# Residual add in the last two batches: token rows by 32x32 turns and DRAM in place of TensorE

## Chip, cores and metric

The kernel runs on one core of a Trainium2 chip. The metric is the device time of one execution in microseconds, the median of the runs shown. All inputs and outputs lie in the chip's DRAM at the start and the end.

## What is computed

For x of shape (8, 3136, 256), a filter in the frequency domain is applied along the sequence, and a low-rank mixer and a two-layer channel network with a residual follow:

```
X = rfft(x, axis=1);  y = irfft(X * (filt_r + i*filt_i), n=3136, axis=1)
yt = y.transpose(0, 2, 1)                      # (8, 256, 3136)
u  = y + (yt @ U @ V).transpose(0, 2, 1)       # U: 3136x32, V: 32x3136
out = u + relu(u @ w_ch1) @ w_ch2              # 256 -> 1024 -> 256, fp32 out
```

The change concerns the first `u +` of the last line.

## The kernel before, in words

**Layout of u.** Stage `s4` leaves u of a batch in the tile `ut[b]`, 128 partitions x (2 halves of the model dimension) x 3136 tokens, in fp16: the model dimension lies on the partitions. The first layer wants it so. The output, and so the residual, wants tokens on the partitions.

**Channel network.** The 8 x 3136 tokens are cut into 49 groups of 512 (`Group`, number n from 0 to 48); a group may straddle two batches (its `seg` list). `mm1(gr, t)` (L487) makes hidden tile t of 8: two matmuls of 512 columns into a PSUM bank of tag "m", and ScalarE applies the relu (L490). `mm2(gr, t)` (L510) does four matmuls of 256 columns into `gr.pc`, a bank of tag "o" (there are two of them). Two values of t finish one block of 128 tokens; on the second, `residual` (L502) adds u to the same PSUM block with two matmuls of 128 columns that take a piece of `ut` as the weights and the identity as the moving operand: this turns u and adds it at once. After two blocks (t = 3 and t = 7) VectorE (DVE) copies the bank into `och` (L517); after t = 7 GpSimd's queue (POOL) stores 512 KB to the output (L522), and in the last group the SP queue stores each half (L519).

**Order of work.** The program order is written out by hand. The main loop makes 392 steps, step 8n+t being `mm1(groups[n], t)`, then `mm2(groups[n-1], t)`, then whatever generators `plan[8n+t]` lists. The residual and the copy of group n thus come in the steps of group n+1. After the loop there are eight more `mm2` for group 48, without `mm1`. `plan` holds the preparation of batch b, spread over the steps in which batch b-1 is in the channel network:

- `f1s`: the first transform; in the steps before group 37 for the last batch.
- `mids`: 13 items, each one a matmul `pz` (L383, L385) into a bank of tag "z" (four of them), a DVE multiply with the filter into `uv` (L391), after every second item a DVE subtract and add (L395, L396), and, three items later, a matmul `pe` on `uv` (L344, function `s3`), a ScalarE cast into `e` (L354) and, for every second pair, a store to DRAM (`ct<-e`, L363, SP queue). For batch 7 items 7 to 12 have their `pz` in steps 297, 299, 301, 303, 305 and 307; the `pe` of items 7 to 9 come in steps 303, 305 and 307, those of items 10 to 12 in steps 310, 311 and 312.
- `loads`: the three parts of `ct` come back as `eb` (L415, SP queue), for batch 7 in steps 309, 310 and 315.
- `ranks`: a chain of small matmuls and four DVE copies (L437), steps 314 to 319.
- `s4s`: matmuls `pu` (L455) on `eb`, cast into `ut` by DVE (L462) and ScalarE (L460), steps 322 to 334 for batch 7.

Each engine's queue and the SP queue run in program order, and semaphores release them. Group 37 starts at step 296; batch 6 starts inside group 36, batch 7 inside group 42 (448 tokens of batch 6, 64 of batch 7). So in groups 37 to 41 the preparation of batch 7 runs beside the network, and in groups 42 to 48 nothing does.

Of the kernel before, what the change touches and what calls it, by code (L numbers as in the profile page):

```python
# [10 lines left out]
F16 = mybir.dt.float16  # L11
# [7 lines left out]
DM = 256  # L19
RANK = 32  # L20
NH = 1024
GT = 512
NG = NB * SEQ // GT

# [53 lines left out]
def kernel(  # L80
# [11 lines left out]
    nc = tc.nc  # L92
# [15 lines left out]
    sb = ctx.enter_context(tc.tile_pool(name="sb", bufs=1))  # L108
    ps = ctx.enter_context(tc.tile_pool(name="ps", bufs=2, space=bass.MemoryType.PSUM))

    def bank(tag, name, dtype=F32):

        return ps.tile([128, 512 if dtype == F32 else 1024], dtype, tag=tag, bufs=4 if tag == "z" else 2, name=name)

    def dram(t, off, dims):
        return bass.AP(tensor=t, offset=off, ap=[list(d) for d in dims])
# [88 lines left out]
    tu = eb[0:RANK, 0:12, :].rearrange("p r d -> p (r d)")  # L205
    tu0 = cst.tile([RANK, NR], F16)

    def u_hat():
        for n in range(8):
            pu = bank("zmzo"[n % 4], "puh")  # L210
            for i in range(4):
                j = 4 * n + i
                nc.tensor.matmul(pu[0:RANK, 98 * i:98 * i + 98], usb[:, j, :], ws[:, j * 98:j * 98 + 98],
                                 start=(i == 0), stop=True, skip_group_check=True)
            copy = nc.vector.tensor_copy if n % 2 else nc.scalar.copy
            copy(tu.rearrange("p (k c j) -> p k c j", c=4, j=32)[:, :, :, 4 * n:4 * n + 4],
                 view(pu[0:RANK], 0, [[1, 24], [24, 4], [98, 4]]))
            copy(view(tu0, 32 * (n // 2 % 2) + 8 * (n // 4) + 4 * (n % 2), [[1, 4], [16, 2]]), view(pu[0:RANK], 96, [[98, 4], [1, 2]]))
# [42 lines left out]
    def unread(p, n, size=512):  # L261
        for _ in range(n):
            nc.tensor.matmul(p[:, 512 - size:512], m64[:, 0:128], m64[:, 0:size], start=True, stop=True, skip_group_check=True)
# [154 lines left out]
    def rank(b):  # L418
        ph = bank("z", "ph")
        for i in range(24):  # L420
            c = i % 4
            nc.tensor.matmul(ph[32 * c:32 * c + 32, 0:DM], uh[:, i + (3 if b == 0 and i > 21 else 1), :], e3[b, i // 4][:, i % 4, :],  # L422
                             start=(i < 4), stop=(i >= 20 and c != 0))
            if b == 0 and i == 19:
                yield
        nc.tensor.matmul(ph[0:32, 0:DM], uh[:, 0, :], e3[b, 6], start=False, stop=True)
        hp = sb.tile([128, DM], F16, tag="hp", bufs=1, name="hp")
        nc.scalar.copy(hp, ph[:, 0:DM])
        if b:
            yield  # L430
        pk = bank("z", "pk")
        nc.tensor.matmul(pk[:, 0:DM], kr, hp, start=True, stop=True)
        h1 = sb.tile([RANK, DM], F16, tag="h1", bufs=2, name="h1")
        nc.scalar.mul(h1, pk[0:32, 0:DM], 2 / 49)  # L434
        yield
        for g in range(4):
            nc.vector.tensor_copy(eb[0:32, 16 * g:16 * g + 16, :],  # L437
                                  bass.AP(tensor=h1.tensor, offset=h1.offset, ap=[[h1.ap[0][0], 32], [0, 16], [1, DM]]))
            yield
# [4 lines left out]
    def s4(b):  # L444
        ut[b] = sb.tile([128, 2, NQ, NR], F16, tag="ut", bufs=2, name="ut")
        for n in range(8):
            g = 2 * (n % 4) + n // 4
            for dh in range(2):
                tag = (("m", "o"), ("z", "z"))[n % 2][dh] if b == 0 else "z"
                pu = bank(tag, "pu")  # L450
                if b == 0:
                    unread(pu, 1, 120)
                d = slice(128 * dh, 128 * dh + 128)
                for i in range(8):
                    nc.tensor.matmul(pu[:, NQ * i:NQ * i + NQ], eb[:, 8 * n + i, d], sv[:, 8 * g + i, :],  # L455
                                            start=(i == 0), stop=True, skip_group_check=True)
                dst = ut[b][:, dh, :, 8 * g:8 * g + 8]
                src = pu[:, 0:8 * NQ].rearrange("p (r q) -> p q r", q=NQ)
                if dh and (b == 0 or n % 2):
                    nc.scalar.copy(dst, src)  # L460
                else:
                    nc.vector.tensor_copy(dst, src)  # L462
                yield
# [13 lines left out]

    groups = [Group(n) for n in range(NG)]

    def utv(b):  # L480
        return ut[b].rearrange("p h q r -> p h (q r)")

    def mm1(gr, t):
        ph = bank("m", "phh")
        for b, t0, o, n in gr.seg:
            for dh in range(2):
                nc.tensor.matmul(ph[:, o:o + n], w1sb[:, dh, 128 * t:128 * t + 128], utv(b)[:, dh, t0:t0 + n],  # L487
                                 start=(dh == 0), stop=(dh == 1), skip_group_check=True)
        h = sb.tile([128, 512], F16, tag="h16", bufs=17, name="h16")
        nc.scalar.activation(h, ph, RELU)  # L490
        gr.h.append(h)

    def residual(gr, o, i):
        last = []
        for b, t0, so, n in gr.seg:
            a, z = max(so, 128 * i), min(so + n, 128 * i + 128)
            for dh in range(2):
                if a < z:
                    p = a - 128 * i
                    last.append((o[p:p + z - a, 128 * dh:128 * dh + 128], utv(b)[:, dh, t0 + a - so:t0 + z - so], dh))  # L500
        for d, w, dh in last:
            nc.tensor.matmul(d, w, idn, start=False, stop=(dh == 1), skip_group_check=True)  # L502

    def mm2(gr, t):
        i, half = t // 2, t % 2
        if t % 4 == 0:
            gr.pc = bank("o", "pc")
        o = gr.pc[:, 256 * (i % 2):256 * (i % 2) + 256]
        for tt in range(4 * half, 4 * half + 4):
            nc.tensor.matmul(o, gr.h[tt][:, 128 * i:128 * i + 128], w2sb[:, tt, :],  # L510
                             start=(tt == 0), stop=False, skip_group_check=True)
        if half:
            residual(gr, o, i)
        if t % 4 == 3:
            if t == 3:
                gr.och = sb.tile([128, 4, DM], F32, tag="och", bufs=2, name="och")
            nc.vector.tensor_copy(gr.och[:, i - 1:i + 1, :], gr.pc.rearrange("p (j d) -> p j d", d=DM))  # L517
            if gr.n == NG - 1:
                nc.sync.dma_start(dram(out.tensor, (gr.n * GT + 128 * (i - 1)) * DM, [[DM, 128], [128 * DM, 2], [1, DM]]),  # L519
                                  gr.och[:, i - 1:i + 1, :])  # L520
            elif t == 7:
                nc.gpsimd.dma_start(dram(out.tensor, gr.n * GT * DM, [[DM, 128], [128 * DM, 4], [1, DM]]), gr.och)  # L522


    S = [8 * (b * SEQ // GT) for b in range(NB)] + [8 * NG]
    plan = [[] for _ in range(8 * NG)]

    def deal(gen, count, a, z):
        for i in range(count):
            plan[max(0, int(a + i * (z - a) / count))].append(gen)  # L530
# [6 lines left out]
    mids = [mid(0, "o")] + [mid(b) for b in range(1, NB)]  # L537
    ranks = [rank(b) for b in range(NB)]
    s4s = [s4(b) for b in range(NB)]

    u_hat()
    u_ordered()
# [48 lines left out]
    for b in range(1, NB):  # L591
        a, z = S[b - 1], S[b]
        e = z - (17 if b == 1 else 20 if b < 6 else 22)
# [8 lines left out]
        if b + 1 < NB:  # L602
            for c in range(4):
                plan[a + (9 + 2 * c if b == 1 else 1 + 4 * c)].append(later_x(b + 1, c))
            deal(f1s[b + 1], 16, a + (21 if b == 1 else 10), z - (13 if b == 1 else 20))

    for n, gr in enumerate(groups):
        for t in range(8):
            mm1(gr, t)
            if n:  # L610
                mm2(groups[n - 1], t)
            for gen in plan[8 * n + t]:
                next(gen, None)
    for t in range(8):
        mm2(groups[-1], t)
# [30 lines left out]
```

## Time and profile before

| what | value |
|---|---|
| median of 3 runs | 520.44 us (519.37 to 521.15) |
| the profiled execution | 522.24 us, of which span 520.5 us |
| TensorE clock granted (mean) | 0.993 of full speed |
| TensorE matmuls (PE) busy | 497.2 us, 96% of the span |
| TensorE weight loads (PEld) busy | 355.4 us, 68% |
| VectorE (DVE) busy | 352.3 us, 68% |
| ScalarE (ACT) busy | 377.1 us, 72% |
| GpSimd (POOL) busy | 80.7 us, 15% |
| DMA moved | 88.22 MB, mean 170 GB/s |

Busy time is the union of an engine's instructions over the span of one profiled execution. Matmuls are pipelined: the duration shown for one is longer than the time after which the next can start, so the distance between starts is the better measure of what a matmul takes. Weight loads (PEld) overlap matmuls. In answers of the trace the first number of a line is the start in us from the beginning of the span, the second the length; brackets give the idle time before it and what ended it. The group numbers and steps above are matched to times by the shapes of the matmuls (group 42's `mm1` is cut into 448 and 64 columns).

### The profile page before, as it was taken

To read this page: it belongs to the slowest core of one execution; us is meant where nothing else is said; L and a number is where in the kernel's file an instruction comes from. 1 tells how busy PE (TensorE), PEld (TensorE's weight loads), DVE (VectorE), ACT (ScalarE), POOL (GpSimd) and SP (SyncE) were. 2 spreads that over 40 slices of the span, in tenths; PEclk is the share of its full clock that TensorE was granted. 3 is DMA by queue.
4 is the path that set the end of the run, shared out by engine and by line. 5 is a ranking of instruction groups with operands and counts; after the bars stand their busy time and mean duration, and the time that the engine had idled before them with its cause. 6 is when DMAs were issued, how large, how long until landed. Compare 5 with 4: busy or idle time off the path is not lost.

```text
span 520.5 us, 11966 instructions
## 1 busy us (share of the span) xinstructions
PE 497.2 (96%) x4852; PEld 355.4 (68%) x4852; DVE 352.3 (68%) x469; ACT 377.1 (72%) x704; POOL 80.7 (15%) x122
## 2 busy tenths in 40 slices
PE   4887899999999999999999999899999999999997
PEld 4545556776767776777767777577667766776665
DVE  5886698588847974788747974689745995621112
ACT  6875779767985789668976799467985677666662
POOL 6662010111010120111010110012010010101110
PEclk9998999999999999999999999899999999999999
DMA  8997846758685586828684597618875136212113
GB/s 194 179 216 175 151 110 188 234 198 171 181 265 206 117 222 207 273 87 185 180 275 180 130 236 218 239 42 196 235 232 199 62 134 189 107 42 83 81 42 122
DMA packets 67375, 88.22 MB, mean 170 GB/s; under 512 B 4835, under 2 KB 51875, under 8 KB 67320
## 3 DMA queue, kind: packets, MB, share of 16 engines
q0 software_dynamic: 14704, 41.58, 30.8%
q1 hardware_dynamic: 52616, 45.88, 28.8%
q8 instruction: 38, 0.62, 0.5%
q14 instruction: 17, 0.14, 0.1%
HBM read 55.20 MB, written 47.78 MB: 198 GB/s over the span
## 4 chain that ended last, share of the span: by engine, by line
PE 82%; DMA 8%; DVE 4%; ACT 2%; issue 1%; POOL 1%; SPq 0%; POOLq 0%; DVEq 0%; ACTq 0%
PE pc L510 31%; PE phh L487 30%; PE pu L455 5%; PE pc L502 4%; PE pf L249 4%; PE pe L344 4%; PE pz L383 3%; DVE uv L391 2%; DMA ct<-e 2%; DMA w2sb<-in_moe_w_ch_dram 2%; DMA x<-in_x_dram 2%; DMA eb<-ct 2%; PE ph L422 1%; DMA fab<-in_filt_i_dram 1%; POOL x L127 1%
## 5 line engine op out<-in xcount | busy, mean ns | idle before, releaser
L490 ACT ACTIVATE h<-phh 128x512 f16<-128x512 f32 x392 | 235.9, 603 | 90.3 <-PE phh L487 88.8
L510 PE MATMUL pc<-w2sb,h 128*128 128x256 f16 x1568 | 234.9, 273 | 0.4 <-DMA w2sb<-in_moe_w_ch_dram 0.4
L487 PE MATMUL phh<-ut,w1sb 128*128 128x512 f16 (+7 forms) x896 | 233.9, 353 | 0.4 <-DVE ut L462 0.4
L510 PEld LDWEIGHTS <-h 128*128 128x128 f16 x1568 | 151.7, 97 | 91.8 <-issue 1.5
L517 DVE COPY och<-pc 128x512 f32<-128x512 f32 x98 | 67.6, 690 | 99.5 <-PE pc L502 98.2
L391 DVE TENSOR_TENSOR uv<-pz,fab 128x1024 f16<-128x1024 f32 (+1 forms) x104 | 120.8, 1179 | 12.6 <-PE pz L383 10.4
L522 POOL DMA_DIRECT2D out_dram<-och x48 | 39.0, 813 | 408.2 <-DVE och L517 392.5
L487 PEld LDWEIGHTS <-w1sb 128*128 128x128 f16 x896 | 77.5, 97 | 19.2 <-issue 1.5
L354 ACT CAST e<-pe 128x512 f16<-128x512 f32 x96 | 56.5, 591 | 19.4 <-PE pe L344 18.8
L462 DVE CAST ut<-pu 128x392 f16<-128x392 f32 x92 | 48.8, 560 | 23.8 <-PE pu L455 22.2
L254 ACT CAST asb<-pf 98x512 f16<-98x512 f32 x96 | 57.2, 598 | 0.2
L502 PE MATMUL pc<-idn,ut 128*128 128x128 f16 (+1 forms) x400 | 54.2, 220 | 0.0
L437 DVE COPY eb<-h 32x4096 f16<-32x4096 f16 x32 | 38.2, 1232 | 14.2 <-ACT h L434 14.1
L455 PE MATMUL pu<-sv,eb 97*128 97x49 f16 x1024 | 40.8, 188 | 4.8 <-DMA eb<-ct 4.8
L344 PE MATMUL pe<-uv,m 128*128 128x512 f16 (+1 forms) x117 | 41.3, 371 | 2.4 <-DVE uv L391 1.3
L455 PEld LDWEIGHTS <-eb 97*128 97x128 f16 x1024 | 37.8, 98 | 6.2 <-DVE eb L437 3.1
L502 PEld LDWEIGHTS <-ut 128*128 128x128 f16 (+1 forms) x400 | 38.2, 98 | 5.4 <-issue 0.8
L383 PE MATMUL pz<-a,m 128*128 128x512 f16 x96 | 36.2, 379 | 1.1 <-DVE a L310 1.0
L249 PE MATMUL pf<-x,ws 98*98 98x256 f16 x192 | 36.7, 273 | 0.0
L395 DVE TENSOR_TENSOR uv<-uv 64x1024 f16<-64x1024 f16 (+1 forms) x49 | 30.9, 630 | 1.7
L396 DVE TENSOR_TENSOR uv<-uv 64x1024 f16<-64x1024 f16 (+1 forms) x49 | 30.8, 628 | 0.7
L249 PEld LDWEIGHTS <-ws 98*98 98x98 f16 x192 | 22.4, 125 | 9.1 <-issue 0.4
(78 smaller groups left out, 225.8 us busy)
## 6 DMA issues: line engine op xcount, KB each, us to landing
out_dram<-och POOLq DMA_DIRECT2D x48, 512.0 KB, 3.8
ct<-e SPq DMA_DIRECT2D x47, 256.0 KB
eb<-ct SPq DMA_DIRECT2D x46, 256.0 KB
x<-in_x_dram POOLq DMA_DIRECT2D x28, 392.0 KB, 7.8
ct<-asb SPq DMA_DIRECT2D x24, 384.0 KB
a<-ct SPq DMA_DIRECT2D x18, 512.0 KB
x<-in_x_dram POOLq DMA_DIRECT2D x4, 384.0 KB, 8.0
ws<-ws SPq DMA_DIRECT2D x1, 600.2 KB
```

The lines of the kernel that those rows point to most:

```text
L249: nc.tensor.matmul(pf[0:98, 256 * s:256 * s + 256], ws[:, (8 * c + j) * 98:(8 * c + j + 1) * 98], t[:, j, :], start=(s == 0), stop=True, s ...
L254: nc.scalar.copy(dst, src)
L344: nc.tensor.matmul(pe[:, 0:n], w, uv[:, f, o:o + n], start=(f == 0), stop=(b > 0 or f == 1))
L354: nc.scalar.copy(t[:, 2 * (i % 2):2 * (i % 2) + 2, :].rearrange("p k d -> p (k d)"), pe)
L383: nc.tensor.matmul(pz, a2m, src[:, k:k + 2, :].rearrange("p k d -> p (k d)"), start=True, stop=True)
L391: nc.vector.tensor_mul(uv[:, :, o:o + n], zin, fin)
L455: nc.tensor.matmul(pu[:, NQ * i:NQ * i + NQ], eb[:, 8 * n + i, d], sv[:, 8 * g + i, :], start=(i == 0), stop=True, skip_group_check=True)
L487: nc.tensor.matmul(ph[:, o:o + n], w1sb[:, dh, 128 * t:128 * t + 128], utv(b)[:, dh, t0:t0 + n], start=(dh == 0), stop=(dh == 1), skip_gro ...
L490: nc.scalar.activation(h, ph, RELU)
L502: nc.tensor.matmul(d, w, idn, start=False, stop=(dh == 1), skip_group_check=True)
L510: nc.tensor.matmul(o, gr.h[tt][:, 128 * i:128 * i + 128], w2sb[:, tt, :], start=(tt == 0), stop=False, skip_group_check=True)
L517: nc.vector.tensor_copy(gr.och[:, i - 1:i + 1, :], gr.pc.rearrange("p (j d) -> p j d", d=DM))
```

## The change

For groups 37 to 48 `residual` is not called. In its place a generator `turn_u` runs in steps 8n, 8n+1, 8n+2 and 8n+5 of the group itself: DVE turns the 32x32 blocks of u (one instruction of 128x512 for each half of the model dimension, six smaller ones in group 42); the SP queue writes the four 32-partition strips to a DRAM tensor of 256 KB in 512-byte pieces, so that token rows are whole there; and the SP queue reads it back as 128 token rows into `gr.tu`. DVE's copy at the end of each half group becomes an add of `gr.pc` and `gr.tu`. The tiles use the slots of tags "asb" and "x", which the last batches no longer need.

```
+FIRST_TURNED = 37
...
+    def turned(gr):
+        return gr.n >= FIRST_TURNED
+
+    def turn_u(gr):
+        t = sb.tile([128, 4, 4, 2, 32], F16, tag="asb", bufs=4, name="tu")
+        for dh in range(2):
+            for b, t0, o, n in gr.seg:
+                j, z = o // 32, (o + n) // 32
+                while j < z:
+                    k = min(z, j + 4 - j % 4) if j % 4 or z - j < 4 else z - z % 4
+                    src = utv(b)[:, dh, t0 + 32 * j - o:t0 + 32 * k - o]
+                    if k - j < 4:
+                        dst = t[:, j % 4:j % 4 + k - j, j // 4, dh, :]
+                        src = src.rearrange("p (c e) -> p c e", e=32)
+                    else:
+                        dst = t[:, :, j // 4:k // 4, dh, :].rearrange("p c g e -> p g c e")
+                        src = src.rearrange("p (g c e) -> p g c e", c=4, e=32)
+                    nc.vector.transpose(dst, src)
+                    j = k
+            yield
+        td = nc.dram_tensor(f"tu_{gr.n}", (128, 4 * DM), F16, kind="Internal")
+        for a in range(4):
+            nc.sync.dma_start(dram(td, DM * a, [[4 * DM, 32], [128 * DM, 4], [1, DM]]),
+                              t[32 * a:32 * a + 32].rearrange("i c g h e -> i c (g h e)"))
+        yield
+        gr.tu = sb.tile([128, 4, 4, 2, 32], F16, tag="x", bufs=4, name="tur")
+        nc.sync.dma_start(gr.tu.rearrange("p a g h e -> p (a g h e)"), td.ap())
+        yield
...
             nc.tensor.matmul(o, gr.h[tt][:, 128 * i:128 * i + 128], w2sb[:, tt, :],
-                             start=(tt == 0), stop=False, skip_group_check=True)
-        if half:
+                             start=(tt == 0), stop=(tt == 7 and turned(gr)), skip_group_check=True)
+        if half and not turned(gr):
             residual(gr, o, i)
...
-            nc.vector.tensor_copy(gr.och[:, i - 1:i + 1, :], gr.pc.rearrange("p (j d) -> p j d", d=DM))
+            if turned(gr):
+                nc.vector.tensor_add(gr.och[:, i - 1:i + 1, :].rearrange("p g (h a e) -> p (g h) a e", h=2, a=4),
+                                     gr.pc.rearrange("p (f a e) -> p f a e", f=4, a=4),
+                                     gr.tu[:, :, i - 1:i + 1].rearrange("p a g h e -> p (g h) a e"))
+            else:
+                nc.vector.tensor_copy(gr.och[:, i - 1:i + 1, :], gr.pc.rearrange("p (j d) -> p j d", d=DM))
...
+    turns = [turn_u(gr) for gr in groups]
...
+    for gr in groups:
+        if turned(gr):
+            for i in range(4):
+                plan[8 * gr.n + (0, 1, 2, 5)[i]].append(turns[gr.n])
```

## The prediction

> **What bounds the kernel now.** I read the page's busy shares first, then the timeline by engine, the windows, and the DMA queue's timeline. The page (busy time; the chain that ended last, by engine):
>
> ```profile
> PE 497.2 (96%) x4852; PEld 355.4 (68%) x4852; DVE 352.3 (68%) x469; ACT 377.1 (72%) x704; POOL 80.7 (15%) x122
> ...
> PE 82%; DMA 8%; DVE 4%; ACT 2%; issue 1%; POOL 1%; SPq 0%; POOLq 0%; DVEq 0%; ACTq 0%
> ```
>
> From 390 to 517 us the timeline shows no idle bracket on PE: what PE sheds there is worth its full time, until something makes it wait. Two steps of group 48 (timeline of PE), the first with a residual, the second without:
>
> ```profile
> 506.01 0.60 PE L487 MATMUL phh<-ut,w1sb 128*128 128x512 f16 x2
> 506.44 0.60 PE L510 MATMUL pc<-w2sb,h 128*128 128x256 f16 x4
> 506.88 0.28 PE L502 MATMUL pc<-idn,ut 128*128 128x128 f16 x2
> 506.99 0.60 PE L487 MATMUL phh<-ut,w1sb 128*128 128x512 f16 x2
> 507.42 0.60 PE L510 MATMUL pc<-w2sb,h 128*128 128x256 f16 x4
> 507.86 0.60 PE L487 MATMUL phh<-ut,w1sb 128*128 128x512 f16 x2
> ```
>
> Starts count: 506.99 - 506.01 = 0.98 us, 507.86 - 506.99 = 0.87 us. A residual pair costs PE 0.11 us, not the 0.28 shown.
>
> DVE, 68% over all, is full where the change first adds to it. Windows: groups 37, 38 and a late one (columns: length, then busy us of PE, PEld, DVE, ACT, POOL, clock, DMA):
>
> ```profile
> 416.50:424.50 8.00, 8.00 (x60) 5.37 (x59) 7.59 (x11) 6.02 (x12) 0.75 (x1) 1.00 0.38 132
> 424.50:433.40 8.90, 8.90 (x66) 5.83 (x64) 7.88 (x10) 6.73 (x13) 0.75 (x1) 1.00 0.45 153
> ...
> 482.90:490.30 7.40, 7.40 (x59) 5.15 (x57) 1.38 (x2) 4.78 (x9) 0.75 (x1) 1.00 0.17 71
> ```
>
> The timeline of DVE there: after the copy at 420.32 (idle 0.18 before it) there is no gap until 432.57, the end of the add that finishes items 11 and 12.
>
> ```profile
> 420.32 0.69 DVE L517 COPY och<-pc 128x512 f32<-128x512 f32 x1 [0.18 <-PE pc L502]
> ...
> 431.89 0.68 DVE L396 TENSOR_TENSOR uv<-uv 64x1024 f16<-64x1024 f16 x1
> 433.68 0.69 DVE L517 COPY och<-pc 128x512 f32<-128x512 f32 x1 [1.10 <-PE pc L502]
> ```
>
> PE uses that result at 433.47, in step 311: 0.90 us to spare. The SP queue in the same stretch:
>
> ```profile
> 428.56 1.94 SPq L415 DMA_DIRECT2D eb<-ct  x2
> 433.31 0.37 SPq L363 DMA_DIRECT2D ct<-e  x1
> 433.76 1.16 SPq L415 DMA_DIRECT2D eb<-ct  x2
> 435.59 0.37 SPq L363 DMA_DIRECT2D ct<-e  x1
> 440.26 1.15 SPq L415 DMA_DIRECT2D eb<-ct  x2
> ```
>
> The last load waited for the write before it to land (435.96 to 440.26, 4.3 us); DMA falls silent at 443.5, 2.1 us after its issue, and PE needs it at 445.10. In the preparation before this one that load was late:
>
> ```profile
> 333.10 0.59 PE L455 MATMUL pu<-sv,eb 97*128 97x49 f16 x16 [2.01 <-DMA eb<-ct]
> ```
>
> **Part 1, removed: -5.5 us.** Eleven groups lose 8 residual matmuls and group 42 loses 10: 98, or 49 pairs. A group lasts 7.39 us (the copies at 483.17 and 490.56) and 8 x 0.867 = 6.94 without pairs, so 0.112 a pair: 49 x 0.112 = 5.5. ACT (4.78 of then 6.94 us) does not become the bound. The Trainium skill (TensorE: Matmul & The Clock Gate, Back-to-back issue gap) gives about 81 ns per matmul of 128 columns in a stream of weight loads and matmuls; by it the 98 would free 7.9 us. The trace's 0.11 per pair contradicts it here.
>
> **Part 2, DVE copy to add: 0.** L517's 128x512 takes 691 ns, L391's multiply of a PSUM and an fp16 operand 692 for the same shape; the add is taken the same.
>
> **Part 3, the turns on DVE: +2.2 us of PE waiting.** No row shows a 32x32 turn. At two elements per cycle L395's 64x1024 takes 686 ns, so 128x512 some 0.42 us; at one per cycle L517's takes 0.69; at half of that 1.22 (L391's 1024 elements). I take 0.70, as a pure one-per-cycle pass; the ends 0.42 and 1.22 stay for the range. The Trainium skill (VectorE: DVE Perf Modes, The three transpose paths) has 311 ns for 128x128; my estimate from it, with 384 more elements at 0.96 per ns, is 0.71. Two turns a group are 1.4 us of DVE. Groups 42 to 48 have 6.0 of 7.4 us idle: hidden (group 42's six small ones, some 2 us, too). Groups 40 and 41 have 2.7 and 4.8 idle: hidden, casts of `ut` late by up to 0.6 (1.4 less the 0.79 idle before the first), with four "z" banks as cover. In groups 37 and 38 nothing hides them. DVE order puts four turns (0.71 each with the step between) ahead of the add of items 11 and 12: 2.84, less the 0.18 idle, is 2.66. That add ends at 435.23, while PE, 0.44 ahead by four pairs, wants it at 433.03: 2.2 us of waiting, with some 0.1 each already paid at items 7 (ready 423.56 + 1.28, wanted 424.79) and 9 within it. At 0.42 per turn the sum is 1.1; at 1.22 it is 4.3. Behind it DVE catches up: the copy at 438.78 had 4.41 us idle, more than group 39's turns.
>
> **Part 4, the SP queue: +1.0 us.** Per group it gets four writes and a load (0.37 to 0.5 us each) and two new waits, for the turns and for its own writes. Behind them stand `ct<-e` and `eb<-ct` of batch 7, on which PE's `pu` waits. Group 38's writes wait for its second turn (431.95); so the loads of step 309, issued at 428.56 before, go at 433.5; then the load of group 38 waits for its writes (2.6 us, the mean of SP's ten waits on `ct<-e` in the trace, 25.6 us, to 4.3): 436.5 to 438.3; the last `ct<-e` leaves at 438.4 to 440.2 instead of 435.59. It lands 2.6 to 4.3 later, behind group 39's writes on the queue; the last `eb<-ct` is issued at 441.7 to 444.5, and with 1.15 and 2.1 it lands at 445.0 to 447.8. PE wants it at 445.10 + 2.2 less eight or nine pairs (0.95) = 446.35. So 0 to 1.5; the 2.01 us row above, with landing 3.1 after issue, points up: I take 1.0, and 0 to 4.6 for the range (6.6 us from the write to the issue, as there).
>
> **Part 5, the trip through DRAM: 0.** From a group's first step: DVE is free at 0.9 (its copy), turns 1.4, writes issued 1.6, landing 3.0, load issued 0.4, landing 2.3: it lands at 9.6. The add comes at 10.4, the end of step 8n+11; the new wait holds DVE, and behind it casts and the next turns. PE waits only past 13.2, since the second "o" bank gives it four more steps. Group 48 has no `mm1` behind it: first add at 8 x 0.867 + 4 x 0.435 = 8.7, second at 10.4; a load that lands by 9.7 delays the first alone, a later one the end, one for one. POOL's stores (0.17 to 0.19 of DMA) are no obstacle; POOL gets nothing new.
>
> Sum: -5.5 + 2.2 + 1.0 = -2.3. The profiled execution would go from 522.24 (span 520.5) to 519.9; it lies 1.8 above the median of the runs, and so I apply the same difference to 520.44: **518.1 us**. A measurement here can tell 0.3% (1.6 us) from no change: faster is below 518.9, slower above 522.0.
>
> **Rivals.**
> - *The load of `eb` binds harder.* Part 4 at 2.5 to 4.6 instead of 1.0: 519.6 to 521.7. For it: the 2.01 us wait above; against: no `a` or x loads compete in this stretch.
> - *Turns at half rate, 1.22 us.* 5.5 - 4.3 - 1.0 = 0.2: 520.2. Nothing in the trace speaks for it.
> - *Fast turns, free queue.* 0.42 us and part 4 at 0: 5.5 - 1.1 = 4.4: 516.0. For it: `eb` has 1.6 us to spare now.
> - *Slower: the trip outlasts its cover.* With 2.0 for the issues, 5.2 for the writes (longest such wait of SP on `ct<-e`) and 4.5 for the load (328.58 to 333.10) the trip is 13.5 us. DVE then paces two groups: (13.5 + two adds, 1.4) / 2 = 7.45 against 6.94, 0.5 x 6 = 3.0 lost in groups 43 to 48, and group 48's load lands at 14.4, 4.7 late: 518.1 + 7.7 = 525.8. It decides from a trip of about 12.5 us, where the end alone is 3.7 late. Against it: DMA is at 0.17 in this stretch.
> - *More is freed than PE's spacing shows*, the mechanism under the skill's figure: the two weight loads (97 ns each) of a pair were on the path. 49 x 0.195 = 9.6: 514.0. The 0.11 us between steps speaks against it.
>
> **Chances.** Forecast (517.1 to 518.9) 0.44; fast turns 0.09; more freed 0.02; `eb` 0.21; half rate 0.06; the trip 0.14, and `eb` beyond 4.9 us 0.04. Faster 0.55, same 0.27, slower 0.18. The range, 515.5 to 522.2, leaves out most of the trip and the ends.
>
> **What would show it.** Steps of 0.867 throughout in groups 43 to 48; turns near 0.70 us; a wait of PE on DVE `uv` near step 311 of about 2 us; a wait of `pu` on `eb<-ct` near step 322 of about 1; the trip landing near 9.6 us, with no idle time of PE on `pc` or of DVE on the load over 1 us. I am wrong if turns differ much from 0.7, if PE's wait at item 11 is absent, or if DVE waits for the load group after group.

## The result and the profile after

The changed kernel takes 515.62 us (median of 6 runs, 514.55 to 516.85); the kernel before, run beside it, 520.03 (6 runs, 517.71 to 521.50). The ratio is 0.9931 with a 95% interval of 0.9903 to 0.9958, that is 3.6 us less (2.2 to 5.0); the two medians alone differ by 4.4. The forecast was 2.3 us less.

The profiled execution takes 516.43 us, span 514.6. Its span is 5.9 us shorter than the one of before, but 2.4 of that lie ahead of the first changed instruction: step 296 begins at 413.60 instead of 415.99, and in eight of the kernels run below, all with the same instructions up to there, it begins anywhere from 411.3 to 414.9. The traced execution of before lost 3.8 us by itself in steps 224 to 231 (12.64 us against 8.85 after): there stands the 2.01 us wait of `pu` at 333.10 that the prediction shows, with the granted clock at 0.50 behind it. So spans are not compared below but the **stretch**, from the first matmul of step 296 to the start of the last DVE instruction: 100.69 us before, 96.97 after, 3.7 less, which agrees with the ratio. The stretch is read from one trace of each kernel.

The page after, busy time and chain:

```profile
PE 490.5 (95%) x4754; PEld 349.6 (68%) x4754; DVE 366.2 (71%) x497; ACT 377.1 (73%) x704; POOL 80.6 (16%) x122
...
PE 81%; DVE 8%; DMA 4%; issue 1%; ACT 1%; SPq 0%; POOL 0%; DVEq 0%; POOLq 0%
```

PE lost its 98 matmuls, and DVE went from 4% to 8% of the chain: somewhere PE now waits for it. (The lines moved: L488 is `mm1`, L544 `mm2`, L345 `pe`, L456 `pu`, L515 the turn, L552 the add.) Late groups, timeline of PE:

```profile
490.38 0.59 PE L488 MATMUL phh<-ut,w1sb 128*128 128x512 f16 x2
...
491.25 0.59 PE L488 MATMUL phh<-ut,w1sb 128*128 128x512 f16 x2
...
492.12 0.59 PE L488 MATMUL phh<-ut,w1sb 128*128 128x512 f16 x2
```

Every step is now 0.87 us, and a group 6.95 instead of 7.39. The timeline of DVE ahead of item 11, and PE's line that waits for it:

```profile
428.25 0.69 DVE L515 STREAM_TRANSPOSE tu<-ut 128x512 f16<-128x512 f16 x1
428.86 0.65 DVE L552 TENSOR_TENSOR och<-pc,tur 128x512 f32<-128x512 f32 x1
...
431.38 0.69 DVE L397 TENSOR_TENSOR uv<-uv 64x1024 f16<-64x1024 f16 x1
```

```profile
432.12 0.39 PE L345 MATMUL pe<-uv,m 128*128 128x512 f16 x1 [1.33 <-DVE uv L397]
...
443.59 0.57 PE L456 MATMUL pu<-sv,eb 97*128 97x49 f16 x16 [0.23 <-issue]
```

The first wait is the one forecast for step 311, at 1.33 us. The second stands where `eb` was forecast to be late; its bracket names no cause, that of the same wait in run 3 has the DMA `eb<-ct`. The SP queue between them:

```profile
428.97 1.76 SPq L520 DMA_DIRECT2D tu<-tu  x4
430.77 1.18 SPq L416 DMA_DIRECT2D eb<-ct  x2
432.27 0.35 SPq L524 DMA_DIRECT2D tur<-tu  x1
...
440.55 1.16 SPq L416 DMA_DIRECT2D eb<-ct  x2
```

Group 38's writes leave at 428.97 to 430.73 and its load at 432.27: they landed within 1.5 us. And the end, timeline of DVE:

```profile
509.11 0.69 DVE L552 TENSOR_TENSOR och<-pc,tur 128x512 f32<-128x512 f32 x1 [1.34 <-DMA tur<-tu]
510.57 0.69 DVE L552 TENSOR_TENSOR och<-pc,tur 128x512 f32<-128x512 f32 x1 [0.77 <-PE pc L544]
```

Group 48's first add waits for its load, the last one for PE: the trip does not reach the end. The 1.34 us are idle time of DVE; without the wait the add would start 0.28 us earlier (run 6 below).

### The profile page after: what moved, and what is told of

It reads as the page before. It is cut to its first block, busy times and chain, and to the rows that moved or that the text cites. A ratio compares the mean times of both kernels' runs of the same rounds, so it can differ in the third digit from the quotient of the medians.

```text
span 514.6 us, 11909 instructions
## 1 busy us (share of the span) xinstructions
PE 490.5 (95%) x4754; PEld 349.6 (68%) x4754; DVE 366.2 (71%) x497; ACT 377.1 (73%) x704; POOL 80.6 (16%) x122
## 4 chain that ended last, share of the span: by engine, by line
PE 81%; DVE 8%; DMA 4%; issue 1%; ACT 1%; SPq 0%; POOL 0%; DVEq 0%; POOLq 0%
PE pc L544 31%; PE phh L488 30%; DVE uv L392 5%; PE pu L456 5%; PE pf L250 4%; PE pe L345 4%; PE pz L384 3%; PE pc L536 3%; DMA w2sb<-in_moe_w_ch_dram 2%; PE ph L423 1%; DVE uv L397 1%; DMA eb<-ct 1%; DVE uv L396 1%; DMA ct<-e 1%; DVE och L556 1%
## 5 line engine op out<-in xcount | busy, mean ns | idle before, releaser
L544 PE MATMUL pc<-w2sb,h 128*128 128x256 f16 x1568 | 233.7, 272 | 1.2 <-DMA w2sb<-in_moe_w_ch_dram 1.2
L488 PE MATMUL phh<-ut,w1sb 128*128 128x512 f16 (+7 forms) x896 | 233.3, 352 | 0.4 <-DVE ut L463 0.4
L544 PEld LDWEIGHTS <-h 128*128 128x128 f16 x1568 | 151.7, 97 | 91.8 <-issue 1.5
L488 PEld LDWEIGHTS <-w1sb 128*128 128x128 f16 x896 | 78.9, 97 | 19.8 <-issue 1.5
L556 DVE COPY och<-pc 128x512 f32<-128x512 f32 x74 | 51.0, 689 | 44.4 <-PE pc L536 43.5
L552 DVE TENSOR_TENSOR och<-pc,tur 128x512 f32<-128x512 f32 x24 | 16.5, 689 | 39.8 <-PE pc L544 37.3
L345 PE MATMUL pe<-uv,m 128*128 128x512 f16 (+1 forms) x117 | 41.3, 371 | 3.6 <-DVE uv L392 1.5
L456 PE MATMUL pu<-sv,eb 97*128 97x49 f16 x1024 | 40.5, 187 | 3.3 <-DMA eb<-ct 3.1
L456 PEld LDWEIGHTS <-eb 97*128 97x128 f16 x1024 | 37.7, 98 | 4.8 <-DVE eb L438 3.4
L536 PE MATMUL pc<-idn,ut 128*128 128x128 f16 (+1 forms) x302 | 40.8, 219 | 0.0
L536 PEld LDWEIGHTS <-ut 128*128 128x128 f16 (+1 forms) x302 | 28.8, 98 | 3.9 <-issue 0.6
```

The source lines that it names most:

```text
L345: nc.tensor.matmul(pe[:, 0:n], w, uv[:, f, o:o + n], start=(f == 0), stop=(b > 0 or f == 1))
```

## The experiments

The edits are against the changed kernel; "..." marks what is left out of them.

**1. Removal alone.**

```
-            if turned(gr):
+            if False:
                 nc.vector.tensor_add(...
...
-        if turned(gr):
+        if False:
             for i in range(4):
```

> Leaves out the residual of groups 37 to 48 altogether (no matmuls, no turns, no trip; the copy stays a copy). The stretch from the first matmul of step 296 to the start of the last DVE instruction was 100.69 us before and is 96.97 after. Theory A (the 49 pairs free 5.5 us, and what is missing from that is DVE's backlog from four turns at item 11): no wait of PE at item 11, stretch 95.1 to 95.5, time about 5.3 us under before. Rival B (the pairs free less, and little is lost elsewhere): stretch 96.3 to 97.0, time no better than the change.

Measured: 513.63 us, ratio 0.9890 (0.9875 to 0.9906); stretch 95.10; no wait of PE at item 11. The 49 pairs free 5.59 us, and theory A stands. The change gives back 1.87 of them.

**2. Turns without the trip.**

```
-        td = nc.dram_tensor(f"tu_{gr.n}", (128, 4 * DM), F16, kind="Internal")
-        for a in range(4):
-            nc.sync.dma_start(...
+        gr.tu = t
         yield
-        gr.tu = sb.tile([128, 4, 4, 2, 32], F16, tag="x", bufs=4, name="tur")
-        nc.sync.dma_start(...
```

> Turns and add stay, the trip through DRAM is left out (the add reads the turned tile directly, so the rows it adds are in the wrong places). Theory A: the wait of PE at item 11 stays at 1.2 to 1.4 us; at most the 0.2 us before the first pu goes; stretch 96.5 to 97.0. Rival C (the SP queue and the DMA cost something, as part 4 of the prediction had with 1.0 us): stretch under 96.2.

Measured: 515.20 us, ratio 0.9938 (0.9917 to 0.9959); stretch 96.59; the wait at item 11 is 1.32, the one before `pu` is gone. Against run 1 the turns cost 1.49 us by the stretch; against the change the trip costs 0.38. The times do not show the second (0.9938 and 0.9931), but the starts of the steps place both: step 311 lasts 1.08 us in run 1, 2.58 here and 2.59 in the change; step 322, with the first `pu`, 1.29 in runs 1 and 2 and 1.67 in the change. These two steps hold the whole 1.87. (The brackets show less, 1.32 and 0.23, since they count from the shown end of the matmul before.) Step 322 takes 1.71 and 1.68 in runs 5 and 6, which have the change's instructions up to there.

**3. From group 38 on.**

```
-FIRST_TURNED = 37
+FIRST_TURNED = 38
```

> Group 37 keeps its residual on PE, groups 38 to 48 are turned: two turns (1.25 us of DVE) fewer ahead of item 11, four pairs (0.45 us) given back. Theory A: PE's wait at item 11 falls from 1.33 to 0 to 0.2 us, stretch 96.0 to 96.4, about 0.8 us better than the change. Rival B: the wait is not of the turns' making and stays near 1.3; stretch about 97.4.

Measured: 514.25 us, ratio 0.9909 (0.9895 to 0.9923); stretch 96.16; PE's wait at item 11 fell under what the timeline marks on matmuls (0.2 on the weight load), and 0.25 for `eb` remained. Two turns fewer were enough. By the stretch it is 0.8 us better than the change; the intervals of the two ratios overlap, so the times alone do not show it.

**4. Each turn twice.**

```
-                    nc.vector.transpose(dst, src)
+                    for _ in range(2):
+                        nc.vector.transpose(dst, src)
```

> Each turn is made twice, with the same result. Theory A: in groups 37 and 38 four more turns of 0.62 to 0.69 us stand ahead of item 11: PE's wait there grows by 2.5 to 2.7, from 1.33 to 3.8 to 4.1 (a part of it perhaps at items 7 and 9); groups 43 to 47 stay at 6.95 us each, since DVE has 3.5 us a group to spare there; the last group's trip starts 1.3 later, its first add comes too late by as much and the end moves by 0.4 to 0.8. Stretch 99.8 to 100.4, time near that of before. Rival B (DVE is not what holds PE): stretch under 98.

Measured: 518.92 us, ratio 0.9991 (0.9976 to 1.0007); stretch 100.92. PE waits 1.06 us at item 7 (step 303) and 3.00 at item 11, 4.06 together as expected; groups 43 to 47 stay at 6.95. The stretch grew by 3.95 us, more than expected, the waits by 2.73. The windows around the second wait (length, busy us of PE, PEld, DVE, ACT, POOL, then clock, DMA share, GB/s) show where some of the rest went:

```profile
428.00:430.90 2.90, 2.90 (x21) 1.82 (x19) 2.87 (x5) 2.36 (x5) 0.00 (x0) 1.00 0.05 17
430.90:433.90 3.00, 0.05 (x1) 0.00 (x0) 2.95 (x4) 0.31 (x1) 0.00 (x0) 0.90 0.33 87
433.90:435.00 1.10, 1.05 (x3) 0.40 (x3) 1.07 (x2) 0.43 (x1) 0.09 (x1) 0.50 0.94 231
435.00:436.00 1.00, 1.00 (x5) 0.59 (x4) 0.96 (x3) 0.67 (x2) 0.67 (x1) 0.50 1.15 287
```

The granted clock is 0.50 from 433.31 to 436.72, so for 2.77 us after the wait, in which PE does half as much (a matmul of 512 columns every 0.43 us instead of 0.22). An estimate from this is 1.4 us lost; the wait ahead of `pu` (0.38) is gone here.

**5. Parts four steps later, groups 43 to 48.**

```
-                plan[8 * gr.n + (0, 1, 2, 5)[i]].append(turns[gr.n])
+                plan[8 * gr.n + ((4, 5, 6, 7) if gr.n > 42 else (0, 1, 2, 5))[i]].append(turns[gr.n])
```

> In groups 43 to 48 each of the four parts of turn_u comes four steps later or so (steps 8n+4, +5, +6, +7 instead of 0, 1, 2, 5), 3.5 us later for the turns; groups 37 to 42 as in the change. Theory A (part 5 of the prediction: PE is held only past 13.2 us of a group's first step, group 48 pays one for one past 9.7): the loads of groups 43 to 47 land at about 12 to 13, DVE waits 1.5 to 3 us for each, PE for none of them, 6.95 us a group as before; group 48 ends 2.5 to 3.5 late. Stretch from step 296 to the last DVE instruction 99.5 to 100.5 (96.97 in the change). Rival D (a late load holds PE in every group): 8.0 us or more a group from 43 on, stretch over 102.

Measured: 529.98 us, ratio 1.0187 (1.0148 to 1.0226); stretch 112.7. Theory A failed: from group 44 on a group takes 9.0 to 10.0 us, 9.4 in the mean, and PE is held four times, for 1.6 to 2.3 us, by DVE's add. Rival D has the size, but the timeline of DVE shows another reason than lateness:

```profile
476.25 0.69 DVE L552 TENSOR_TENSOR och<-pc,tur 128x512 f32<-128x512 f32 x1 [5.43 <-DMA tur<-tu]
476.86 1.30 DVE L515 STREAM_TRANSPOSE tu<-ut 128x512 f16<-128x512 f16 x2
478.08 0.65 DVE L552 TENSOR_TENSOR och<-pc,tur 128x512 f32<-128x512 f32 x1
485.98 0.69 DVE L552 TENSOR_TENSOR och<-pc,tur 128x512 f32<-128x512 f32 x1 [7.25 <-DMA tur<-tu]
```

At steps 8n+4 and 8n+5 the turns of group n stand behind the first add of group n-1 on DVE, and that add waits for the load of n-1. The turn, its trip and the next add are then a chain that each group must run through alone: 485.98 - 476.25 = 9.7 us. In the change the turn stands ahead of that add, and a trip may span two groups.

**6. Later in the plan, same place on DVE.**

```
-                plan[8 * gr.n + (0, 1, 2, 5)[i]].append(turns[gr.n])
+                plan[8 * gr.n + ((2, 2, 3, 6) if gr.n > 42 else (0, 1, 2, 5))[i]].append(turns[gr.n])
```

> As the run with parts of turn_u four steps later in groups 43 to 48, but at steps 8n+2, +2, +3 and +6: later in the plan than in the change, still ahead of the add of step 8n+3 on DVE. Theory E (what cost 9.0 us a group with four steps was not the lateness but that the turn came behind the add that waits for the load before: turn, trip and add then form a chain of one group): DVE takes the turns at the same moment as in the change, since it waits for nothing between the last add and them; 6.95 us a group, DVE waits of 1.5 us at most for the load, stretch 96.8 to 97.3. Theory A2 (each step later costs part of the cover): 0.9 us or more a group, stretch over 101.

Measured: 514.61 us, ratio 0.9926 (0.9904 to 0.9949); stretch 96.99, the change's own; every add from group 43 on starts within 0.02 us of the change's, except the one that waits for the last load, 0.28 earlier. Theory E stands: for these two steps, what counts is which instruction a turn stands behind, not the step that it is written in.

**7. Group 38's turns behind item 12.**

```
-                plan[8 * gr.n + (0, 1, 2, 5)[i]].append(turns[gr.n])
+                plan[8 * gr.n + ((3, 3, 4, 7) if gr.n == 38 else (0, 1, 2, 5))[i]].append(turns[gr.n])
```

> All of groups 37 to 48 turned, but group 38's two turns come in step 307 behind item 12 instead of in steps 304 and 305. Theory A: PE's wait at item 11 falls to 0 to 0.2, as with group 37 left out; but the load of group 38 is late, DVE waits for it 2 to 3 us at step 315, and the copies into eb and the casts of ut behind it cost PE 0 to 0.6. Stretch 95.6 to 96.4, i.e. 0.6 to 1.3 better than the change. Rival D: the new wait of DVE costs PE as much as the old one, stretch 97 or more.

Measured: 520.47 us, ratio 1.0016 (0.9993 to 1.0040); stretch 100.91. The wait at item 11 went as theory A has it, but DVE's wait for the load (timeline of DVE) was 9.0 us, not 2 to 3, and it held PE for 3.74 (timeline of PE):

```profile
443.87 0.69 DVE L552 TENSOR_TENSOR och<-pc,tur 128x512 f32<-128x512 f32 x1 [9.00 <-DMA tur<-tu]
```

```profile
444.62 0.60 PE L544 MATMUL pc<-w2sb,h 128*128 128x256 f16 x4 [3.74 <-DVE och L552]
```

The writes left at 433.12 to 434.89; the load stood behind two pairs of `eb` loads and a `ct` write on the SP queue, left at 438.51 and took 5.4 us to land, with the DMA share at 0.88 to 1.05. The clock was at 0.50 after this wait too, from 445.82 to 449.23. Rival D holds, by more than it said (97 or more).

**8. Groups 34 and 35 as well.**

```
-FIRST_TURNED = 37
+FIRST_TURNED = 38
-        return gr.n >= FIRST_TURNED
+        return gr.n >= FIRST_TURNED or gr.n in (34, 35)
```

> Turned are groups 34, 35 and 38 to 48: eight pairs more than from 38 on, in steps where DVE waits for PE a good part of the time, as in groups 40 and 41. Theory A: 0.9 us less PE work before step 288 for 0 to 0.4 us of waiting; 0.5 to 0.9 us under the version from 38 on, 5.1 to 5.6 us under before. Rival B: DVE's backlog from 402 us on is full and anything put ahead of it costs PE; no gain over the version from 38 on.

Measured: 521.03 us, ratio 1.0028 (1.0003 to 1.0053). From the last cut `mm1` of group 30 (the one that a batch boundary cuts in two) to step 296 it takes 65.4 us, 59.3 in the change, though eight pairs (0.9 us) are gone there. Neither theory had the cause; timeline of PE, then of SP:

```profile
403.54 0.61 PE L384 MATMUL pz<-a,m 128*128 128x512 f16 x1 [4.74 <-DMA a<-ct]
```

```profile
392.07 0.34 SPq L524 DMA_DIRECT2D tur<-tu  x1
397.94 1.76 SPq L520 DMA_DIRECT2D tu<-tu  x4
399.74 0.45 SPq L331 DMA_DIRECT2D a<-ct  x1
```

The SP queue used to run far ahead: the loads of `a` for batch 7 left at 387.73 in run 3. Here they stand behind the writes of group 35, which wait for its turns, and leave some 12 us later. The granted clock was 0.50 from 400.97 to 407.80; half of the 4.26 us of it that follow the wait, 2.1 us, is an estimate of what that cost, and with the 4.74, less the pairs, it gives 5.9 of the 6.1.

Step 322 lasts 2.53 us here (PE waits 1.08 for `eb`), 1.70 in run 3 with the same instructions from step 296 on. What sets this wait is not shown.

**9. Group 35 with its DMAs behind the loads of `a`.**

```
-FIRST_TURNED = 37
+FIRST_TURNED = 38
...
-        return gr.n >= FIRST_TURNED
+        return gr.n >= FIRST_TURNED or gr.n == 35
...
-                plan[8 * gr.n + (0, 1, 2, 5)[i]].append(turns[gr.n])
+                plan[8 * gr.n + ((0, 1, 4, 7) if gr.n == 35 else (0, 1, 2, 5))[i]].append(turns[gr.n])
```

> Turned are groups 35 and 38 to 48; group 35's writes and load come in steps 284 and 287, behind the loads of a (step 283) on the SP queue. Theory F (the 4.7 us that PE waited for a when groups 34 and 35 were turned came from the SP queue: turns and trips ahead of the loads of a): PE waits for a not at all or under 0.3, the stretch from step 296 stays at 96.0 to 96.5, and the time is 0 to 0.5 under the version from 38 on. Rival B (DVE's backlog from 402 us on holds PE): a wait on uv or pz of DVE's making of 1 us or more.

Measured: 515.25 us, ratio 0.9925 (0.9901 to 0.9950); stretch 96.41. The loads of `a` leave at 385.40, and PE does not wait for `a` at all: theory F stands. Group 34 keeps its residual here, so what its turns alone did to run 8 is not told apart. From the last cut `mm1` of group 30 to the last DVE instruction it takes 155.30 us, the shortest of the complete kernels (before 160.03, the change 156.32, run 3 155.88). Of the 0.58 between it and run 3, 0.39 is a loss that run 3 had ahead of step 296, where it has the change's instructions. The rest is 0.44 that group 35's four pairs gave, less 0.25 for a longer step 322 (1.95, 1.70 in run 3); the times do not separate it from run 3.

**10. The trip on GpSimd's queue.**

```
-            nc.sync.dma_start(dram(td, DM * a, ...
+            nc.gpsimd.dma_start(dram(td, DM * a, ...
...
-        nc.sync.dma_start(gr.tu.rearrange(...
+        nc.gpsimd.dma_start(gr.tu.rearrange(...
```

> The change with its writes and loads issued from GpSimd's queue instead of SP's. Theory A: the wait at item 11 stays at 1.3; the 0.4 us lost around step 322, which the run without the trip did not have, goes, since the loads of eb no longer stand behind the trip; GpSimd's issues are slower (0.8 us against 0.35 to 0.5), so that group 48's trip is 1 to 2 us longer and its end 0 to 1 late. Stretch 96.6 to 97.6. Rival G (DMA traffic, not the queue's order, cost the 0.4): it stays, stretch 97.0 to 98.0.

Measured: 516.18 us, ratio 0.9941 (0.9920 to 0.9963); stretch 97.2. PE's wait at the first `pu` is gone (step 322 lasts 1.29), but DVE waits 4.7 us for one load and PE then 0.45 for a cast of `ut`; the last add comes directly behind its late neighbour. Inconclusive: the queue's order and the traffic are not told apart by it.

## Why the prediction was right, and where its sizes were off

**Right in kind.** The forecast's mechanism held: PE's full gain, one wait at item 11 in step 311 made by four turns on a full DVE, a small loss around `eb`, and a trip that fits. The 518.1 was 2.3 under the 520.44 that was known then; measured is 3.6 less (2.2 to 5.0), by the stretch 3.7. The forecast had given 1.4 us too much back to waiting: 3.2 instead of 1.87. The time itself, 515.62, lies below the forecast's own 517.1 to 518.9 and only 0.12 above the low end of the range, and before ran 0.41 faster than known; that it fell inside is partly luck.

**Part 1, -5.5:** run 1 has -5.59. The step of 0.112 us a pair was the right measure. The Trainium skill's figure of about 81 ns per matmul (TensorE: Matmul & The Clock Gate, Back-to-back issue gap), which made it 7.9, did not hold for these pairs: 5.59 us over 98 is 57 ns each.

**Part 2, 0:** the add takes 689 ns, as the copy did.

**Part 3, +2.2, is the larger term that was mis-sized:** 1.49. The turn takes 0.66 to 0.71 us, 0.69 in the mean, as taken. But a turn adds less than its length: 428.25 to 428.86 is 0.61, 426.50 to 427.14 is 0.64, since the next instruction starts before the turn's end. I had charged 0.71 each. The multiplies ahead of a second turn also took a little less room (427.14 to 428.25 is 1.11, 1.18 ahead of a copy before), and the add of items 11 and 12 ended 1.90 us later, not 2.66, counted from the copy of step 295 (15.73 us before, 17.63 after). Less the 0.90 to spare and plus the 0.44 that PE is ahead, 1.90 gives 1.44, and step 311 is 1.50 longer than in run 1. Step 303 is as long as before (1.41): the 0.1 us that item 7 was to cost did not show. Runs 3 and 4 show the dose: two turns fewer, 0.2 us of waiting left; four more, 2.73 more.

**Part 4, +1.0, was too dear:** 0.38 by run 2. Two sizes in it were off and nearly cancelled. Group 38's writes landed within 1.5 us, not in the 2.6 to 4.3 taken from `ct<-e`; but from the issue of the last `ct<-e` to the last `eb` loads it took 4.9 (435.69 to 440.55), with group 39's writes issued in between, where 2.6 to 4.3 was given. So the last `eb` loads left at 440.55, which is 442.94 counted with the step 296 of before, inside the 441.7 to 444.5 given. With the prediction's own 3.25 for issue and landing that makes 0.4 us of waiting for a PE that is ready at 443.37.

What failed is the choice of 1.0 out of 0 to 1.5, taken up because of the 2.01 us row. That row does not stand for the kernel: of the other eleven traces, with the same instructions there, seven lose nothing in steps 224 to 231 (8.85 or 8.86 us against the 12.64), two 0.1 to 0.2 and two 0.4 and 0.7. (It also belongs to batch 5; batch 6, the preparation before this one, has no wait in that trace.) The size of the wait is not fixed, though: step 322 lasts 1.95 us in run 9 and 2.53 in run 8.

**Part 5, 0:** right for the place where the change puts the turns. The trip from the first turn to the landing is 8.4 us in group 48 (500.74 to 509.11), 8.7 was reckoned. It landed 9.2 us after the group's first step, and DVE's idle time on the load was over 1 us twice, 1.13 in group 39 and 1.34 in group 48, with no wait of PE. But the reason was incomplete: 13.2 us of cover holds only while the turn stands ahead of the add before it on DVE, as runs 5 and 6 show.

**The rivals.** `eb` late, half-rate turns and a trip that outlasts its cover did not come in the change. Fast turns had 516.0, the number nearest to 515.62, but not the reason: the turns took 0.69 us, not 0.42. *More is freed* is ruled out by run 1 (5.59 us, not 9.6). The trip did outlast its cover in runs 5 and 7, with the loss that it was feared for, from placements of the same instructions. Nothing here tests turns faster than 0.69 us.

## What to carry to other kernels

Read what a removed matmul is worth from the distance between starts in steps with and without it, not from its shown length. Before adding work to an engine that is idle on average, find the stretch where it has no gap and the next engine's margin there; keeping one group of the twelve out of it was worth 0.8 us of the stretch, though its own removed matmuls were lost again. When a trip through a queue is added, look at what it stands behind and what stands behind it: the same twelve trips cost 0.4 us or about 16 (112.7 in run 5 against 96.59 without a trip), by their place in two in-order queues. And look for a wait in a second trace before pricing by it: the row that raised part 4 was one execution's.

## What the hardware showed

- In or behind waits of PE of 3.00 us (run 4) and 3.74 us (run 7) the granted clock fell to 0.50 for 3.41 us; after waits of 1.33 (the change) and 2.30 us (run 5) it stayed at 1.00. But it fell also behind waits of 2.01 us (before, at 333.81) and 2.15 us (run 5, at 505.96), so the length of the wait alone does not decide.
- In each of the twelve traces the changes of the granted clock lie whole multiples of 3.41 us apart. Cut into stretches of that length, from 300 us on, a stretch with 2.01 us or more of idle PE is followed by 0.50 (2.01 before, 2.15 run 5, 2.18 run 8, 2.21 run 7, 2.36 run 4), one with 1.91 or less is not (1.91 run 4, 1.89 run 5). The 2.30 us fell across two stretches, 1.06 and 1.24. Near 41 us, beside other work, 1.71 was enough in run 1 and 1.91 was not in run 7, so this is no general threshold.
- The Trainium skill (TensorE: Matmul & The Clock Gate, The HAM clock gate) puts the fall at an idle window of about 3.4 us; here 2.01 us of idle time within 3.41 were enough.
- A DVE turn of 128x512 in fp16 takes 0.66 to 0.71 us, but the next instruction starts 0.59 to 0.64 us after its start, whether a PSUM reader or the turn of the other half. Where run 4 makes the same turn again, into the same place, the second starts only 0.70 to 0.75 us after the first.
- A write of 256 KB in 512-byte pieces landed within 1.5 us of its last issue in one place; a load of 256 KB, the SP queue's only transfer then, landed in 2.7 (506.45 to 509.11), and one issued behind `eb` loads and ahead of other writes in 5.4 (run 7).
